# Attention, routed experts and a rational feed-forward layer on one core: gates, weight loads and a pipeline's lag moved

## The chip, the cores and the metric

The kernel runs on one core of a Trainium2 chip. The metric is the device time of one execution in microseconds (us); lower is better. A time is the median of several executions, and one more execution is taken by the hardware profiler.

## The reference

Three layers follow each other on 3072 tokens of 512 numbers, all in fp32.

```python
# 1 attention: chunks of 32 queries see 16 keys to the left, 8 to the right and 8 memory slots
a = softmax(scale * q_c @ k_full.T);  out = a @ v_full
# 2 experts: 8 of them, one per token
logits = x @ w_gate + modality_bias[modality_id]
e_idx = argmax(logits);  gate_w = softmax(logits)[e_idx]
h = maximum(x[mask] @ w1[e], 0);  out[mask] = gate_w[mask, None] * (h @ w2[e])
# 3 feed-forward with a rational function
h = x @ w_in                                   # 512 -> 2048
g = (a0 + a1*h + a2*h*h + a3*h**3) / (1 + |b0|*|h| + |b1|*h*h + 1e-6)
out = g @ w_out                                # 2048 -> 512
```

`w_in` and `w_out` come as float64 and are narrowed on the chip.

## The kernel before, in words

Attention and the router fill the first 150 us. They sort the tokens by expert into slots of 128.

**Experts.** `moe` handles 20 slots as five quads of four slots (512 tokens); I call them the first to the fifth quad (`q` 0 to 4). A quad runs eight steps, `n` 0 to 7, one for each 128 hidden units. In a step TensorE (PE) does 12 products of the first layer (`mm1_quad`, lines 1018 to 1020), ScalarE (ACT) takes the ReLU (`hh`, line 1025) and VectorE (DVE) the low half (`hl`, line 1026); PE then does the 12 products of the second layer of the step before (`mm2_quad`, lines 1035 to 1037). Every fp32 operand is split in a high and a low part, so each product is three matmuls.

While a quad runs, the next one is prepared. POOL gathers its four slots of x (`gather`, line 807) into the buffers `xy`. ACT scales each by the token's gate (`gate_x`, line 907). At `n` = 7 PE transposes the first two of them (`prep_x`, line 1081) ahead of `mm2_quad(6)`, and the other two behind it; ACT and DVE write the result into `xq` (lines 1083 and 1085), which the next quad's first product reads. SP loads the next expert's weights, if the expert changes, in four pairs of 512 KB, one pair in each of four steps (`load_w`, line 820); ACT and DVE split them (`split_w`, lines 917 and 920).

The first and the fourth quad also carry a small extra slot of 32 rows (`k` is not `None`) with an expert of its own: its weights are loaded raw in the steps 0 to 3, two pieces of `w1r` or `w2r` a step, its first layer runs at `n` = 3 (`mm1_small`, line 856) and its second at `n` = 4 (`mm2_small`, line 872).

Beside all this runs the **converter**, which narrows `w_in` and `w_out`, one piece of 128 x 512 at each call of `filler()`. One call issues the end of the last piece (a cast on ACT, line 1326, a subtraction on DVE, line 1327, and for `w_out` two stores from POOL, lines 1329 and 1330), the load of the next piece on SP (line 1313, 512 KB into `wr`, two buffers) and the bits of this piece (line 1259 on ACT and four operations on DVE, lines 1260 to 1263).

The order of all instructions is that of the program text: `manual_schedule` keeps it, and each engine takes its own in that order. Inside a step the text has first `mm1_quad` and the ReLU, then at `n` = 7 the first transposes, then `mm2_quad`, then `at(n)`:

```python
        def at(n):
            if n in FILLERS[q]:
                filler()
            ...                                       # the small slot's loads, load_w
            if n >= NC8 - 2 and len(nxt) > 1:         # NC8 is 8
                for c in nxt[0:2] if n == NC8 - 2 else nxt[2:4]:
                    ex.gate_x(c)
```

**Feed-forward.** `moe2` runs 96 steps, six blocks of 512 tokens by 16 pieces of 128 hidden units. Step `i` has 12 matmuls of the first layer on PE (`mm1`, lines 1402 to 1404), the rational function on ACT and DVE, whose results are `gh` (ACT, line 1438) and `gl` (DVE, line 1444), and the second layer (`mm2`, lines 1459 to 1461), which does nothing for an even piece and 24 matmuls for two pieces after an odd one. `mm2` of step `i - LAG` stands behind `mm1` of step `i`, and `LAG` is 3. A block's sums lie in four PSUM banks and are copied out by `evac` (lines 1467 to 1472) and stored by POOL (line 1474).

Of the kernel before, what the change touches and what calls it, by code (L numbers as in the profile page):

```python
# [13 lines left out]
F32R = mybir.dt.float32r  # L14
# [8 lines left out]
P = 128  # L23
# [322 lines left out]
NC8 = 1024 // P  # L346
# [3 lines left out]
class Router:  # L350
# [137 lines left out]
    def gates(self, lo, hi):  # L488

        V = self.nc.vector  # L490
        a = slice(lo, hi)
        L, g = self.L[:, a], self.v[:, 4, a]
        return [
            lambda: V.reduce_sum(g, L, axis=AX.X),
            lambda: V.tensor_scalar_add(g, g, 1e-9),
            lambda: V.reciprocal(g, g),
        ]
# [605 lines left out]
FILLERS = (range(8), range(6), range(6), (0, 4, 5, 6, 7), range(8))  # L1103


def moe(nc, tc, ex, filler, rows, gp):
    ET = mybir.EngineType
    flags, w1r = ex.flags, ex.w1r
    gate0 = gp.tile([P, QUAD * P], F32, name="gate0")
    small = gp.tile([P, 4, SM], F32, name="small_y")  # L1110

    def quad(q):
        c0 = Q_FIRST + QUAD * q
        nxt = range(c0 + QUAD, c0 + 2 * QUAD) if q + 1 < QUADS else range(S_LAST, S_LAST + 1)
        k = QUAD_SMALL.get(q)
        pieces = {0: (1, 0), 1: (1, 2), 2: (2, 0), 3: (2, 2)}
        loads = {n if k is None else n + 4: x for n, x in pieces.items()}
        part1, part2 = (5, 6) if k is None else (6, 7)
        sx, (sh, sT) = ex.xy[3], [x[:, 0:256] for x in ex.xg[0:2]]
        sT = sT[:, 0:P].rearrange("p (k n) -> p k n", k=4)  # L1120
        hT = ex.xg[0][:, 256:512].rearrange("p (i n) -> p i n", i=2)
        if k is not None:
            e = ex.expert(NS - 1 - k)

        def at(n):

            if n in FILLERS[q]:
                filler()
            if k is not None and n in pieces:
                layer, i = pieces[n]  # L1130
                ex.load(e, layer, range(i, i + 2))
            if n in loads:
                layer, i = loads[n]
                ex.load_w(nxt[0], layer, range(i, i + 2))
            if n == part1:
                ex.split_w(nxt[0], 1, range(2))
            if n == part2:
                ex.split_w(nxt[0], 2, range(2))
            if n == (2 if k is None else 5):
                for c in nxt:  # L1140
                    ex.gather(c)
            if n >= NC8 - 2 and len(nxt) > 1:
                for c in nxt[0:2] if n == NC8 - 2 else nxt[2:4]:
                    ex.gate_x(c)

        for n in range(NC8):
            ps = ex.mm1_quad(n)
            if n == 0 and q == 0:
                ex.mm2(EARLY, 0)
                ex.put(1, ex.turn(1))  # L1150
                ex.mm2(EARLY, 1)
                ex.out(EARLY)
            if n == 1 and q == 0:
                ex.put(EARLY, ex.turn(EARLY))
                ex.gate_row(Q_FIRST, gate0)
            ex.relu_quad(n, ps)
            if n == 0 and q == 0:
                ex.load_w(Q_FIRST, 2)
                ex.split_w(Q_FIRST, 2)
            if k is not None and n == 0:  # L1160
                ex.gather_small(k, sx[:, 0:D_M])
            if k is not None and n == 3:
                ex.prep_x_small(sx, sT)
            if k is not None and n == 4:
                ex.prep_h_small(sh, hT)
            if k is not None and n == 5:
                ex.put_small(k, sx[:, 0:D_M], small)
            if n == NC8 - 1:
                xs = [(c, ex.prep_x(c, c - nxt[0] if len(nxt) > 1 else None)) for c in nxt[0:2]]
                for c, low in xs:  # L1170
                    low()
            if n > 0:
                ex.mm2_quad(n - 1)
            if k is not None and n == 3:
                ex.mm1_small(sT, sh)
            if k is not None and n == 4:
                ex.out_small(k, ex.mm2_small(hT), sx)
            at(n)
        for c in nxt[2:]:
            ex.prep_x(c, c - nxt[0])()  # L1180
        ex.split_w(nxt[0], 1, range(2, 4))
        if q + 1 == QUADS:
            while filler():
                pass
            rows.open()
            for t in range(4):
                rows.load(0, t, w1r[:, t, 0:TB])
            for part in range(3):
                ex.mm1(S_LAST, part)
            ex.hs = ex.w2r[:, 0].rearrange("p (i j n) -> p i j n", i=2, j=4)  # L1190
            ex.relu(S_LAST)
            ex.mm2_quad(NC8 - 1, range(2))
            ex.prep_h(S_LAST, 0)
        ex.mm2_quad(NC8 - 1, range(2, 4) if q + 1 == QUADS else range(QUAD))
        ex.put_quad(c0, gate0 if q == 0 else None)
        ex.split_w(nxt[0], 2, range(2, 4))

    def first_y(t):
        rows.prep(t, w1r[:, t, 0:TB], rows.h, rows.l)

    filler()
    ex.split_w(EARLY, 2)
    for q in range(QUADS):
        quad(q)
    ex.prep_h(S_LAST, 1)
    for t in range(4):
        first_y(t)
    for k in range(SMALL - 1, -1, -1):
        ex.copy_small(k)
    ALL = (ET.PE, ET.Activation, ET.DVE, ET.Pool, ET.SP)  # L1210
    more = nc.values_load(flags[0:1, 2, 0:1], engines=ALL, min_val=0, max_val=1)
    tc.mark_branch_hint_location("more", "LikelyTaken", engines=(ET.PE, ET.Activation))
    for g in range(2):
        ex.mm2(S_LAST, g)
    with tc.If(more == 1, label="more"):
        ex.clear_columns(w1r[:, 0])
        for i in range(Q_FIRST, NN):
            if i == S_LAST or i < S_LAST and (i - Q_FIRST) % QUAD == 0:
                continue
            todo = nc.values_load(flags[0:1, 2, i:i + 1], engines=ALL, min_val=0, max_val=1)  # L1220
            with tc.If(todo == 1):
                e = ex.expert(i)
                for layer in (1, 2):
                    ex.load(e, layer)
                    ex.split_w(i, layer, always=True)
                nc.gpsimd.memset(ex.xg[i % QUAD], 0.0)
                ex.gather(i)
                ex.prep_x(i)()
                for part in range(3):
                    ex.mm1(i, part)  # L1230
                ex.relu(i)
                ex.prep_h(i, 0)
                ex.prep_h(i, 1)
                for part in range(2):
                    ex.mm2(i, part)
                ex.out(i)
                ex.merge(i)
        for t in range(4):
            rows.load(0, t, w1r[:, t, 0:TB])
        for t in range(4):  # L1240
            first_y(t)
    ex.out(S_LAST, y=rows.spare, ps=ex.pb[1])
# [2 lines left out]
DM, DF = 512, 2048  # L1245
NB = 6
TB = 512
LAG = 3
NF = DF // P
NK = DM // P  # L1250
F_MIN = float(np.array(0x38000000, np.uint32).view(np.float32))
# [116 lines left out]
def moe2(nc, tc, rows, wih, wil, wod, consts, out):  # L1368
    with ExitStack() as ctx:
        cp = ctx.enter_context(tc.tile_pool(name="c_c", reuse_waits="tile", bufs=1))  # L1370
        rp = ctx.enter_context(tc.tile_pool(name="c_r", reuse_waits="tile", bufs=2))
        wk = ctx.enter_context(tc.tile_pool(name="c_w", reuse_waits="tile", bufs=2))
# [19 lines left out]
        def prep_y(blk, k):  # L1392
            rows.prep(k, yr.pop((blk, k)), *yT[blk % 2])
# [40 lines left out]
            V.scalar_tensor_tensor(out=u, in0=u, scalar=a0, in1=q, op0=ALU.add, op1=ALU.mult)  # L1434

        def ew_hi(i):
            gh = wk.tile([P, TB], F32R, tag="gh", name="gh", bufs=4)
            A.copy(gh, u_t[i])  # L1438
            g_t[i] = gh

        def ew_lo(i):
            gl = wk.tile([P, TB], F32R, tag="gl", name="gl", bufs=4)
            gh = g_t[i]
            V.tensor_tensor(out=gl, in0=u_t.pop(i), in1=gh.bitcast(F32), op=ALU.subtract)  # L1444
            g_t[i] = (gh, gl)
# [38 lines left out]
        n = len(steps)  # L1484
        for i in range(n + LAG):
            if i < n:
# [8 lines left out]
            if 2 <= i <= n + 1:  # L1495
                ew_lo(steps[i - 2])
            if i >= LAG:
                mm2(*steps[i - LAG])
            if i < n:
                ew_act1(steps[i])  # L1500
            if 1 <= i <= n:
                ew_dve2(steps[i - 1])
                ew_hi(steps[i - 1])
            if i < n:
# [4 lines left out]
                if blk + 1 < NB:  # L1509
                    if f in (4, 6, 9, 11):  # L1510
                        load_y(blk + 1, (f - 3) // 2 - f // 9)
                    if f in (8, 10, 12, 14):
                        prep_y(blk + 1, (f - 8) // 2)
            if i >= LAG and steps[i - LAG][1] == NF - 1:
                evac(steps[i - LAG][0])

# [99 lines left out]
```

## Time and profile before

| | |
|---|---|
| median of 3 runs | 949.23 us (948.18 to 950.88) |
| the profiled execution | 950.31 us |
| its span, first to last instruction | 948.6 us |
| mean granted TensorE clock | 0.996 of full |
| PE busy | 916.0 us, 97% |
| DVE busy | 743.3 us, 78% |
| ACT busy | 546.4 us, 58% |
| POOL busy | 150.9 us, 16% |

Times in rows count from the span's start. A group of instructions with a number in brackets behind it has that much idle time of its engine ahead of it, and the arrow names what ended the idle time. A matmul's end is modelled and its duration overlaps the next one's, so lengths on PE are taken from start to start.

### The profile page before, as it was taken

What the parts mean: (1) busy time and instruction counts of PE and PEld (TensorE: products, weight loads), DVE (VectorE), ACT (ScalarE), POOL (GpSimd) and SP (SyncE); (2) the same over time, 40 slices, a digit from 0 to 9 for tenths busy, and PEclk for the clock granted to TensorE, in tenths of its full rate; (3) what the DMA queues carried; (4) which work ended last, traced back from release to release, by engine and by line L of the source; (5) the groups of instructions that cost most, each with busy time, mean ns of one, the idle gap of its engine ahead of it and who ended that gap; (6) DMA issues with size and microseconds to landing.
All of it is one profiled execution on the core that took longest, in us unless ns stands there. A gap on an engine that the chain in (4) does not pass through costs nothing.

```text
span 948.6 us, 15349 instructions
## 1 busy us (share of the span) xinstructions
PE 916.0 (97%) x5684; PEld 744.7 (79%) x5684; DVE 743.3 (78%) x1244; ACT 546.4 (58%) x913; POOL 150.9 (16%) x198
## 2 busy tenths in 40 slices
PE   6999899999999999999999999999999999999997
PEld 5786578688887778877888888888888888888885
DVE  6777693377767266549999899899999998998884
ACT  3554433243737153257777676777766776767663
POOL 5111221031121043114631000100010010001001
PEclk9999999999999999999999999999999999999999
DMA  8999633459293676556851000100010010001001
GB/s 320 360 386 354 216 101 121 157 167 324 83 339 121 236 225 206 204 189 95 124 65 62 1 23 22 45 12 23 12 45 23 23 45 1 23 1 45 1 1 44
DMA packets 37814, 114.90 MB, mean 121 GB/s; under 512 B 8987, under 2 KB 9119, under 8 KB 34912
## 3 DMA queue, kind: packets, MB, share of 16 engines
q1 hardware_dynamic: 25920, 79.06, 27.1%
q0 software_dynamic: 11488, 33.85, 9.9%
q8 instruction: 46, 0.75, 0.3%
q10 hardware_dynamic: 320, 0.91, 0.3%
q14 instruction: 40, 0.33, 0.1%
HBM read 86.51 MB, written 27.54 MB: 120 GB/s over the span
## 4 chain that ended last, share of the span: by engine, by line
issue 55%; PE 26%; POOL 7%; DMA 6%; DVE 4%; ACT 1%; POOLq 1%; ACTq 0%; DVEq 0%; SPq 0%
POOL od L897 3%; DMA yd<-xy 2%; PE pv L210 2%; PE pa L154 2%; PE hq L1018 2%; POOL out L1474 2%; PE hq L1019 2%; PE hq L1020 2%; DMA wr<-in_moe_w_out 2%; PE pps L188 1%; PE pb L1096 1%; PE pa L949 1%; PE xps L234 1%; PE pb L1035 1%; PE pb L1037 1%
## 5 line engine op out<-in xcount | busy, mean ns | idle before, releaser
L1459 PE MATMUL a<-wo,gh 128*128 128x512 f32 x384 | 149.6, 390 | 1.6 <-ACT gh L1438 1.6
L1461 PE MATMUL a<-wo,gl 128*128 128x512 f32 x384 | 149.6, 390 | 1.3 <-DVE gl L1444 1.3
L1402 PE MATMUL h<-yh,wih 128*128 128x512 f32 x384 | 149.6, 389 | 0.8 <-ACT wf L956 0.8
L1404 PE MATMUL h<-yh,wil 128*128 128x512 f32 x384 | 149.4, 389 | 0.0
L1403 PE MATMUL h<-yl,wih 128*128 128x512 f32 x384 | 149.4, 389 | 0.0
L1460 PE MATMUL a<-wo,gh 128*128 128x512 f32 x384 | 149.4, 389 | 0.0
L1414 ACT ACTIVATE s<-h 128x512 f32<-128x512 f32 x96 | 56.6, 590 | 105.4 <-PE h L1404 105.4
L1421 DVE SCALAR_TENSOR_TENSOR q<-s,ab,q 128x512 f32<-128x512 f32 x96 | 71.8, 748 | 38.0 <-ACT q L1415 38.0
L1474 POOL DMA_INDIRECT out<-o,out_rows x24 | 25.4, 1060 | 426.4 <-ACT o L1470 419.7
L1438 ACT CAST gh<-u 128x512 fp32r<-128x512 f32 x96 | 59.9, 624 | 45.3 <-DVE u L1434 41.4
L1459 PEld LDWEIGHTS a<-wo,gh 128*128 128x128 f32 x384 | 72.1, 188 | 17.3 <-ACT gh L1438 2.5
L1461 PEld LDWEIGHTS a<-wo,gl 128*128 128x128 f32 x384 | 72.0, 187 | 17.0 <-DVE gl L1444 2.1
L1402 PEld LDWEIGHTS h<-yh,wih 128*128 128x128 f32 x384 | 72.0, 188 | 16.0 <-ACT wf L956 1.2
L1404 PEld LDWEIGHTS h<-yh,wil 128*128 128x128 f32 x384 | 72.2, 188 | 15.1
L1460 PEld LDWEIGHTS a<-wo,gh 128*128 128x128 f32 x384 | 72.2, 188 | 14.8
L1403 PEld LDWEIGHTS h<-yl,wih 128*128 128x128 f32 x384 | 72.0, 188 | 14.9
L1416 ACT ACTIVATE u<-h,ab 128x512 f32<-128x512 f32 x96 | 74.9, 780 | 0.0
L1434 DVE SCALAR_TENSOR_TENSOR u<-u,ab,q 128x512 f32<-128x512 f32 x96 | 72.2, 752 | 3.4
L1423 DVE SCALAR_TENSOR_TENSOR u<-u,ab,h 128x512 f32<-128x512 f32 x96 | 71.8, 748 | 3.4
L1432 DVE SCALAR_TENSOR_TENSOR q<-q,ab,s 128x512 f32<-128x512 f32 x96 | 71.6, 745 | 1.7 <-ACT s L1428 1.7
L1427 ACT ACTIVATE s<-q,ab 128x512 f32<-128x512 f32 x96 | 70.1, 730 | 1.1
L1433 DVE SCALAR_TENSOR_TENSOR q<-q,s 128x512 f32<-128x512 f32 x96 | 66.4, 692 | 3.3
(308 smaller groups left out, 1785.9 us busy)
## 6 DMA issues: line engine op xcount, KB each, us to landing
in<-in_qkv SPq DMA_DIRECT2D x22, 560.0 KB
in<-in_qkv SPq DMA_DIRECT2D x22, 556.0 KB
w1r<-in_moe_w SPq DMA_DIRECT2D x20, 512.0 KB
w2r<-in_moe_w SPq DMA_DIRECT2D x20, 512.0 KB
wr<-in_moe_w_in SPq DMA_DIRECT2D x16, 512.0 KB
wr<-in_moe_w_out SPq DMA_DIRECT2D x16, 512.0 KB
wod<-wo POOLq DMA_DIRECT2D x32, 256.0 KB
wo<-wod SPq DMA_DIRECT2D x16, 512.0 KB
```

The lines of the kernel that those rows point to most:

```text
L1402: nc.tensor.matmul(ps, lhsT=wih[k][:, sl], rhs=h[:, k], start=(k == 0), stop=False)
L1403: nc.tensor.matmul(ps, lhsT=wih[k][:, sl], rhs=l[:, k], start=False, stop=False)
L1404: nc.tensor.matmul(ps, lhsT=wil[k][:, sl], rhs=h[:, k], start=False, stop=(k == NK - 1))
L1416: A.activation(u, ps, func=AF.Identity, scale=a3, bias=a2)
L1421: V.scalar_tensor_tensor(out=q, in0=s, scalar=absb1, in1=q, op0=ALU.mult, op1=ALU.add)
L1423: V.scalar_tensor_tensor(out=u, in0=u, scalar=a1, in1=ps, op0=ALU.add, op1=ALU.mult)
L1427: A.activation(s, q, func=AF.Ln, bias=cb)
L1432: V.scalar_tensor_tensor(out=q, in0=q, scalar=cb, in1=s, op0=ALU.add, op1=ALU.mult)
L1434: V.scalar_tensor_tensor(out=u, in0=u, scalar=a0, in1=q, op0=ALU.add, op1=ALU.mult)
L1459: nc.tensor.matmul(ps, lhsT=gh[:, sl], rhs=wo[x][:, 0].bitcast(F32R), start=(x == 0), stop=False)
L1460: nc.tensor.matmul(ps, lhsT=gh[:, sl], rhs=wo[x][:, 1].bitcast(F32R), start=False, stop=False)
L1461: nc.tensor.matmul(ps, lhsT=gl[:, sl], rhs=wo[x][:, 0].bitcast(F32R), start=False, stop=(x == NF - 1))
```

## The change

Four things move. The gates are issued directly behind a ReLU and the next products, no longer at the end of `at(n)`: for quads with a small slot at `n` = 6 (two slots) and, behind the first transposes of `n` = 7, the other two; for quads without one at `n` = 5 and `n` = 6. In `at(n)` the loads of experts' weights come ahead of the converter's call. `LAG` goes from 3 to 4. `gh` and `gl` get six buffers each.

```diff
@@ quad @@
+        gate1 = 5 if k is None else 6
+
+        def gates(cs):
+            for c in cs:
+                ex.gate_x(c)
+
@@ at(n) @@
-            if n in FILLERS[q]:
-                filler()
             if k is not None and n in pieces:
                 layer, i = pieces[n]
                 ex.load(e, layer, range(i, i + 2))
             if n in loads:
                 layer, i = loads[n]
                 ex.load_w(nxt[0], layer, range(i, i + 2))
+            if n in FILLERS[q]:
+                filler()
@@
-            if n >= NC8 - 2 and len(nxt) > 1:
-                for c in nxt[0:2] if n == NC8 - 2 else nxt[2:4]:
-                    ex.gate_x(c)
@@ the loop over n @@
             ex.relu_quad(n, ps)
+            if len(nxt) > 1 and n == gate1:
+                gates(nxt[0:2])
+            if len(nxt) > 1 and n == gate1 + 1 and k is None:
+                gates(nxt[2:4])
@@
                 for c, low in xs:
                     low()
+                if k is not None:
+                    gates(nxt[2:4])
@@ moe2 @@
-LAG = 3
+LAG = 4
-            gh = wk.tile([P, TB], F32R, tag="gh", name="gh", bufs=4)
+            gh = wk.tile([P, TB], F32R, tag="gh", name="gh", bufs=6)
-            gl = wk.tile([P, TB], F32R, tag="gl", name="gl", bufs=4)
+            gl = wk.tile([P, TB], F32R, tag="gl", name="gl", bufs=6)
```

The changed kernel's lines from 1119 on have numbers up to 9 higher. In the rows below `wr` is the converter's raw buffer.

On SP, in the first quad, before, the steps `n` = 2 and `n` = 3:

```order
L1313 DMA wr_2322<-in_moe2_w_in 128x1024
L820 ISA
L820 DMA w2r_93<-in_moe_w2 128x2x512
L820 ISA
L820 DMA w2r_93<-in_moe_w2 128x2x512
L1313 DMA wr_2322<-in_moe2_w_in 128x1024
L820 ISA
L820 DMA w2r_93<-in_moe_w2 128x2x512
L820 ISA
L820 DMA w2r_93<-in_moe_w2 128x2x512
```

Now, from the converter's load of `n` = 1 to that of `n` = 3:

```order
L1322 DMA wr_2322<-in_moe2_w_in 128x1024
L820 ISA
L820 DMA w2r_93<-in_moe_w2 128x2x512
L820 ISA
L820 DMA w2r_93<-in_moe_w2 128x2x512
L1322 DMA wr_2322<-in_moe2_w_in 128x1024
L820 ISA
L820 DMA w2r_93<-in_moe_w2 128x2x512
L820 ISA
L820 DMA w2r_93<-in_moe_w2 128x2x512
L1322 DMA wr_2322<-in_moe2_w_in 128x1024
```

Each pair of the small slot's pieces stands one converter load earlier in SP's queue.

On ACT, in the fourth quad, before, from the ReLU of `n` = 6 (`hh`) to the gates of the next quad's first two slots (`xy_89`, `xy_86`); the rows from 924 to 930 are a branch over a split that is not taken there:

```order
L1025 ACTIVATE hh_1762<-hq 128x512
L1326 CAST wo<-wr 128x512
L1259 ACTIVATE wf<-wr 128x512
L924 TENSOR_LOAD flags
L924 ISA x2
L930 COMPARE_AND_BRANCH
L917 CAST w1h<-w1r 128x4x256 x2
L930 UNCONDITIONAL_BRANCH x2
L907 ACTIVATE xy_89<-xy_89,gate_s 128x512
L834 UNCONDITIONAL_BRANCH
L907 ACTIVATE xy_86<-xy_86,gate_s 128x512
```

Now:

```order
L1025 ACTIVATE hh_1762<-hq 128x512
L907 ACTIVATE xy_89<-xy_89,gate_s 128x512
L907 ACTIVATE xy_86<-xy_86,gate_s 128x512
L1335 CAST wo<-wr 128x512
L1268 ACTIVATE wf<-wr 128x512
```

The gates have passed the converter's two instructions, and a wait for the gathered rows now stands ahead of those.

On PE, at the start of the feed-forward stage, before, the end of the fifth `mm1` (`h_8703`) and the start of the first `mm2` (`a0_8684`):

```order
L1404 MATMUL h_8703<-yh0_4965,wil2_2316 128x512
L1402 MATMUL h_8703<-yh0_4965,wih3_2313 128x512
L1403 MATMUL h_8703<-yl0_4966,wih3_2313 128x512
L1404 MATMUL h_8703<-yh0_4965,wil3_2317 128x512
L1459 MATMUL a0_8684<-wo0_8450,gh_8629 128x512
L1460 MATMUL a0_8684<-wo0_8450,gh_8629 128x512
```

Now, the end of the fifth `mm1` (`h_8699`) and the start of the sixth (`h_8737`):

```order
L1413 MATMUL h_8699<-yh0_4965,wil2_2316 128x512
L1411 MATMUL h_8699<-yh0_4965,wih3_2313 128x512
L1412 MATMUL h_8699<-yl0_4966,wih3_2313 128x512
L1413 MATMUL h_8699<-yh0_4965,wil3_2317 128x512
L1411 MATMUL h_8737<-yh0_4965,wih0_2310 128x512
L1412 MATMUL h_8737<-yl0_4966,wih0_2310 128x512
```

A sixth `mm1` of 12 matmuls stands ahead of the first `mm2`; at the end of the stage, accordingly, three `mm2` follow each other with no `mm1` between them, where two did.

## Rows read from the trace of the kernel before

**Rows 1.** The page, busy time, share and instructions of each engine.
```profile
PE 916.0 (97%) x5684; PEld 744.7 (79%) x5684; DVE 743.3 (78%) x1244; ACT 546.4 (58%) x913; POOL 150.9 (16%) x198
```

**Rows 2.** Waits of PE: line, releaser, us in total, times, longest; feed-forward's second layer.
```profile
PE a L1459 <- ACT gh L1438: 1.6, 2, 0.9
PE a L1461 <- DVE gl L1444: 1.3, 1, 1.3
```

**Rows 3.** PE's timeline and windows, small slots, `n` = 4; columns: busy of engines, PEclk, DMA.
```profile
181.54 1.08 PE L872 MATMUL syp<-w2r,xy 128*32 128x128 f32 x32
184.12 0.65 PE L872 MATMUL syp<-w2r,xy 128*32 128x128 f32 x16 [1.50 <-DMA w2r<-in_moe_w]
...
330.63 1.95 PE L872 MATMUL syp<-w2r,xy 128*32 128x128 f32 x64
...
181.54:190.54 9.00, 6.82 (x77) 4.92 (x76) 2.18 (x5) 2.58 (x6) 0.00 (x0) 0.81 0.25 80
330.63:335.46 4.83, 4.83 (x78) 3.86 (x77) 0.71 (x2) 2.56 (x6) 0.45 (x1) 1.00 0.01 3
```

**Rows 4.** Timeline of SP, first quad, n = 2 and n = 3.
```profile
167.43 0.97 SPq L820 DMA_DIRECT2D w2r<-in_moe_w  x2
...
178.04 0.95 SPq L820 DMA_DIRECT2D w2r<-in_moe_w  x2
```

**Rows 5.** Timeline of PE, ACT and SP, end of the third quad.
```profile
295.23 1.36 PE L1081 MATMUL xps<-ident,xy 128*128 128x128 f32 x8 [1.76 <-ACT xy L907]
...
288.97 0.67 ACT L1259 ACTIVATE wf<-wr 128x512 f32<-128x512 f32 x1 [3.01 <-DMA wr<-in_moe_w_out]
...
280.71 0.35 SPq L1313 DMA_DIRECT2D wr<-in_moe_w_out  x1
```

**Rows 6.** Timelines and a window, end of the fourth quad; the last two rows end the second.
```profile
340.25 1.07 POOL L807 DMA_INDIRECT xy<-xd,src_u  x1 [0.30 <-issue]
...
343.08 0.66 ACT L1326 CAST wo<-wr 128x512 fp32r<-128x512 f32 x1 [0.83 <-DVE wr L1263]
...
344.49 0.34 SPq L1313 DMA_DIRECT2D wr<-in_moe_w_out  x1
...
345.74 1.36 ACT L907 ACTIVATE xy<-xy,gate_s 128x512 f32<-128x512 f32 x2 [0.60 <-DMA xy<-xd,src_u]
...
350.43 0.66 ACT L1259 ACTIVATE wf<-wr 128x512 f32<-128x512 f32 x1 [1.21 <-DMA wr<-in_moe_w_out]
...
352.36 1.64 PE L1081 MATMUL xps<-ident,xy 128*128 128x128 f32 x8 [1.66 <-ACT xy L907]
...
354.66 0.69 DVE L1085 TENSOR_TENSOR xq<-xps,xq 128x512 fp32r<-128x512 f32 x1 [0.20 <-ACT xq L1083]
...
357.90 0.40 PE L1018 MATMUL hq<-xq,w1h 128*128 128x512 f32 x1
...
350.00:375.00 25.00, 23.34 (x100) 19.02 (x99) 15.72 (x27) 10.42 (x18) 7.50 (x13) 0.93 0.63 205
...
251.52 1.12 PE L1081 MATMUL xps<-ident,xy 128*128 128x128 f32 x8
...
255.23 0.39 PE L1018 MATMUL hq<-xq,w1h 128*128 128x512 f32 x1
```

**Rows 7.** Timeline of PE and DVE, start of the feed-forward stage.
```profile
429.49 0.39 PE L1459 MATMUL a<-wo,gh 128*128 128x512 f32 x1
...
437.64 0.39 PE L1402 MATMUL h<-yh,wih 128*128 128x512 f32 x1
...
443.08 0.39 PE L1459 MATMUL a<-wo,gh 128*128 128x512 f32 x1
...
427.66 0.68 DVE L1444 TENSOR_TENSOR gl<-u,gh 128x512 fp32r<-128x512 f32 x1
...
432.48 0.68 DVE L1444 TENSOR_TENSOR gl<-u,gh 128x512 fp32r<-128x512 f32 x1
```

**Rows 8.** Timeline of PE and DVE, end of the feed-forward stage.
```profile
935.40 0.39 PE L1459 MATMUL a<-wo,gh 128*128 128x512 f32 x1
...
941.92 0.39 PE L1461 MATMUL a<-wo,gl 128*128 128x512 f32 x1
```

## The prediction

> **What bounds the kernel now.** I read the page's engine list first. PE is busy 97% of the span and DVE 78% [rows 1], so PE sets the end and only what shortens, lengthens or idles PE counts. So next I read PE's idle groups and, around each, the timelines of PE and of the engine that ended the wait. Behind the router stage three places lose time that an edit of this change touches: the small slot's second layer in the first quad waits for its weights [rows 3, 4]; the transposes at the end of the third and of the fourth quad wait for ACT's gates [rows 5, 6]; the feed-forward stage waits for `gh` and `gl` three times, 2.9 us in all, and never again in its 96 steps [rows 2]. In [rows 7, 8] the reader sees where those three are. The clock is the last thing to see: around the fourth quad's end the granted clock is 0.93 over 25 us [rows 6], so the wait there cost more than its own length.
>
> **Loads ahead of the converter.** The small slot's second layer is 64 matmuls, and from their start to the next transposes PE takes 9.00 us in the first quad and 4.83 in the fourth [rows 3]. The same work, so 4.17 us are lost in the first. The row names 1.50 of them as a wait for `w2r`; the granted clock of that stretch is 0.81 against 1.00, so PE also ran part of it at its lower level, 1.2 GHz, behind the stall [rows 3]. What it waits for is the pair issued at 178.04; the pair before was issued at 167.43 [rows 4]. SP was held between them by the converter's load, which needs a free `wr`. In the order of the change that load stands behind the pair, so the last pair goes out where the one before it did, some 10.6 us earlier; even at the 8.26 us that the longest load of my rows took (280.71 to 288.97) [rows 5] it has landed by 176, ahead of 181.54. **-4.17**, nothing if the pair cannot go earlier. The converter's load comes two issues (1 us) later; it has a step to land, see the slower rival. In the other quads PE waited for no pair: 0.
>
> **Gates, third quad.** PE stood 1.76 us at 295.23 for the gates on ACT, while ACT had idled 3.01 us ahead of 288.97, waiting for a load [rows 5]. The first two gates (1.36 us for two [rows 6]) now go into `n` = 5, where their rows have long landed, and fit into that idle time. **-1.76.** The second quad's boundary took 3.71 us from transpose to first product without a wait (251.52 to 255.23) [rows 6]: 0 there.
>
> **Gates, fourth quad.** The boundary ran from 350.70 (352.36 less 1.66 of wait) to 357.90, 7.20 us against 3.71 undisturbed [rows 6]: 3.49 to win, half of it the wait, half the lower clock behind it. But the gates now stand ahead of the converter's cast on ACT and wait for the gather. The gather was issued at 340.25 and ACT could start at 345.74, until 347.10; the cast had run at 343.08 [rows 6]. So it goes 4.0 later, and with it SP's load, from 344.49 to 348.5. The load took 5.94 to its use at 350.43 [rows 6]; behind that use stand DVE's bits and then the last low half of `xq`, which ended at 355.35, 4.92 behind. If the whole delay is passed on, the use is at 354.4 and the quad starts at 359.3, 1.4 later than before; with the wait comes the lower clock, another 1.8 (3.49 less 1.66): **+3.0** at worst, rounded. If the load is quicker by what a quiet queue may give (use at 351.7, hardly more than 3 us behind its issue), the low half ends at 356.6, and PE starts 1.3 to 1.5 earlier: **-1.5** at best. I take **0**, the middle, as ACT's wait goes and DVE's comes.
>
> The gather of 128 rows took 5.49 us from issue to use (340.25 to 345.74) [rows 6]. The Trainium skill, "DMA: Bandwidth & Descriptors", section "Anatomy of one DMA — SWDGE (gpsimd) path", fits about 2.0 us plus bytes over 436 GB/s per transfer issued from POOL; that makes an estimate of 2.6 us for 256 KB, half of the row. By that rule the gates would be through about when the cast began, the converter would be some 1 us late, and this term -1.5 and the time 938.0. The row decides: 5.49.
>
> **Gates, first quad.** The same reorder, on a boundary that did not wait for gates. Its rows can land late too; if not, the gates' own 1.36 us [rows 6] come ahead of the cast. From 0 to +1.4; I take **+0.2**, since ACT is busy 58% of the span [rows 1] and mostly has the room.
>
> **LAG, start.** From the first `mm2` at 429.49 to the next `mm1` at 437.64 are 8.15 us, and the same 24 matmuls in the next step take 5.44 (437.64 to 443.08) [rows 7]. The 2.71 between are waits for `gh` and `gl` and what follows them. With the sixth `mm1` ahead, 12 matmuls or 2.72 us of the same work are put in front. The first `gl` was there at 432.48 + 0.68 = 433.16 [rows 7]; its first reader is then at 429.49 + 2.72 + 5 x 0.227 = 433.34. A slack of 0.17 only, but it grows: DVE gives one `gl` every 4.82 us (427.66 to 432.48) [rows 7] and PE takes 5.44. **-2.71**; 0.5 less if `gl` is that much late. Each `gh` and `gl` lives a step longer, and six buffers instead of four give that room and one more, so nothing waits for a free one: 0.
>
> **LAG, end.** The last `mm2` from 935.40 to 941.92 took 6.52 us for 23 starts, at 0.2267 each 5.21 [rows 8]: the last results were late. Now another `mm2` stands before it and hides that: **-1.31**. What follows, the copies out and the stores, keeps its length: 0. `evac` comes a step later, on banks that the next block needs a step later too: 0.
>
> **Sum.** -4.17 - 1.76 + 0 + 0.2 - 2.71 - 1.31 = -9.75. The profiled execution took 950.31, so 940.6; it lies 1.08 above the median of 949.23, so **939.5** against the median.
>
> **Rivals.** *Late boundaries.* The fourth quad loses 3.0 and the first 1.4 in place of 0 and 0.2: 943.7. For: ACT's new wait stands ahead of the cast. Against: the load may land sooner. 0.16.
>
> *Early gathers.* The gates' rows lie there when ACT comes, by 343.1, and the converter's load lands in 5 us; then the fourth boundary is undisturbed and gains up to its 3.49: 936.0 to 938.0. Against: the 5.49 us of [rows 6]. 0.09.
>
> *The pair does not move.* If the raw buffer of the last pair is still read when SP comes to it, the 4.17 stay: 943.7. Against: the fourth quad runs the same two layers out of the same buffers without a wait [rows 3]. 0.05. *Two at once*, this and the late boundaries: 947.9, no change that can be told. 0.06.
>
> *Slower: the converter starves.* Its load now stands directly behind a pair of 1 MB. A load had 8.26 us issue to use (280.71 to 288.97), shortly behind pairs, and 5.94 (344.49 to 350.43) with none near [rows 5, 6], 2.32 more. It has a step, 5.44 us [rows 7], and ACT's next ReLU stands behind it; PE needs that only 12 matmuls (2.72) later. So from 8.16 us per load, step after step, PE stops. Over the 13 steps with both, half of 2.32 reaching PE gives 15 us: 954.5. For: one row is already above 8.16. Against: the pairs were ahead of that load before as well, and PE did not stop for it; they come in 13 steps, never together. 0.06.
>
> **How the numbers follow.** Forecast 0.58, its own range 938 to 941.5 (fourth quad -1.5 to +1.5, `gl` 0.5). A measurement can tell about 0.3%, 2.8 us. Faster by more: forecast, late boundaries, early gathers, unmoved pair, 0.88; within it: two at once, 0.06; slower: 0.06. Range 935.8 to 943.8: it takes in all but the last two and the edges.
>
> **What would show it.** Right: in the first quad `syp` runs without a wait for `w2r`, some 4.8 us to the next group; no wait for `xy` at the third quad's transposes; at the fourth's end the gates run at about 345.7 with the cast behind them, and PE waits for `xq`, not for ACT's gates; the start of feed-forward has no wait for `gh` or `gl`, and its last `mm2` takes 5.2. Wrong: a wait of PE for `hh` or for the converter's `wf` in many steps (starving), a wait for `w2r` as before, or `mm2` waiting for `gl` in mid-stage.

## The result: 1.0% faster, 0.9899 of the time before

The changed kernel takes 940.75 us (median of 6 runs, 939.40 to 942.37) against 951.15 of the kernel before in the same comparison; the ratio is 0.9899 (0.9882 to 0.9916), which on the median of 949.23 is 939.6. The profiled execution took 939.40 with a span of 937.8, 10.8 less than before. The page of the kernel after, busy time of each engine:

```profile
PE 911.8 (97%) x5684; PEld 742.7 (79%) x5684; DVE 742.8 (79%) x1244; ACT 547.2 (58%) x913; POOL 149.8 (16%) x198
```

The work is the same as in [rows 1]; PE is busy 4.2 us less, which fits its granted clock (0.999 on average, 0.996 before), and idle 6.6 us less. The waits of PE in what this change touches, kernel after (line, releaser, us, times, longest):

```profile
PE hq L1019 <- DVEq L930: 2.7, 2, 2.3
```

The two groups of [rows 2] are gone, and so are the waits for `w2r` and for ACT's `xy` of [rows 3, 5, 6]; one new group is there: the second matmul of a quad waits for DVE.

**The small slot.** Timeline and window of PE, kernel after, first quad, `n` = 4 (window: length, busy time of PE, PEld, DVE, ACT, POOL, granted clock, DMA share, GB/s):

```profile
181.07 1.95 PE L872 MATMUL syp<-w2r,xy 128*32 128x128 f32 x64
185.90 0.43 PE L964 MATMUL yps<-ident,xy 32*128 32x32 f32 x4
...
181.07:185.90 4.83, 4.83 (x77) 3.86 (x77) 0.71 (x2) 2.56 (x6) 0.00 (x0) 1.00 0.00 1
```

The 64 matmuls run in one piece at full clock, 4.83 us to the next group as in the fourth quad of [rows 3]. SP, kernel after: the last pair of `w2r` is issued at 167.04, where before it was 178.04 [rows 4].

```profile
161.96 0.98 SPq L820 DMA_DIRECT2D w2r<-in_moe_w  x2
166.43 0.35 SPq L1322 DMA_DIRECT2D wr<-in_moe_w_in  x1
167.04 0.95 SPq L820 DMA_DIRECT2D w2r<-in_moe_w  x2
```

**The fourth boundary.** Timelines of POOL, ACT, DVE and PE, kernel after:

```profile
334.11 1.06 POOL L807 DMA_INDIRECT xy<-xd,src_u  x1 [0.30 <-issue]
...
339.15 1.46 ACT L907 ACTIVATE xy<-xy,gate_s 128x512 f32<-128x512 f32 x2 [3.04 <-DMA xy<-xd,src_u]
340.52 0.65 ACT L1335 CAST wo<-wr 128x512 fp32r<-128x512 f32 x1
...
346.19 0.69 ACT L1268 ACTIVATE wf<-wr 128x512 f32<-128x512 f32 x1 [0.91 <-DMA wr<-in_moe_w_out]
...
349.83 1.29 DVE L1085 TENSOR_TENSOR xq<-xps,xq 128x512 fp32r<-128x512 f32 x2 [0.49 <-DVEq L930]
...
348.49 0.39 PE L1018 MATMUL hq<-xq,w1h 128*128 128x512 f32 x1
351.18 0.50 PE L1019 MATMUL hq<-xq,w1h 128*128 128x512 f32 x1 [2.30 <-DVEq L930]
```

The gates wait 3.04 us for the gather on ACT, the cast stands behind them, and the chain of [rows 6] runs later: load, `wf` at 346.19, DVE's bits, the last low halves until 351.12. PE has its transposes and starts the quad at 348.49, but its second matmul reads the low half and waits 2.30. The profile names a branch of DVE (`DVEq L930`) as the releaser; the last low half ended at 351.12, 0.06 ahead of PE's start, and the run filler_behind below shows that it is this that PE waits for.

**The third boundary.** Timelines of SP, ACT and PE, kernel after:

```profile
277.80 0.35 SPq L1322 DMA_DIRECT2D wr<-in_moe_w_out  x1
...
279.73 1.33 ACT L907 ACTIVATE xy<-xy,gate_s 128x512 f32<-128x512 f32 x2
...
282.91 0.66 ACT L1268 ACTIVATE wf<-wr 128x512 f32<-128x512 f32 x1 [0.45 <-DMA wr<-in_moe_w_out]
...
289.29 1.11 PE L1081 MATMUL xps<-ident,xy 128*128 128x128 f32 x8
```

PE's transposes have no wait ahead of them. ACT's gates ran early, but the converter's load also came sooner: ACT waits 0.45 us for it where it waited 3.01 [rows 5]. Which of the two ended PE's wait the experiments must tell.

**Feed-forward.** Timeline of PE, kernel after, its first `mm2`, the `mm1` behind it, and the last `mm2`:

```profile
425.31 0.39 PE L1468 MATMUL a<-wo,gh 128*128 128x512 f32 x1
...
430.80 0.39 PE L1411 MATMUL h<-yh,wih 128*128 128x512 f32 x1
...
925.84 0.39 PE L1468 MATMUL a<-wo,gh 128*128 128x512 f32 x1
...
931.05 0.39 PE L1470 MATMUL a<-wo,gl 128*128 128x512 f32 x1
```

5.49 us in place of 8.15 [rows 7], and 5.21 for the last in place of 6.52 [rows 8].

**Lengths by stage.** PE runs 5684 matmuls in every kernel here, up to feed-forward the same ones in the same order, so I cut all traces at the same matmuls, from start to start: the small slot from the 2251st to the 2321st, the first boundary 2361st to 2441st, the start of the second quad to the 2561st, the third boundary 2741st to 2831st, the fourth 3081st to 3161st, feed-forward's first 96 matmuls (from the 3377th), and its tail from the 5661st to the end of the span. The table has the profiled execution of every run, in us:

| kernel | small slot | 1st boundary | 2nd quad's start | 3rd boundary | 4th boundary | ff start | tail |
|---|---|---|---|---|---|---|---|
| before | 11.99 | 17.52 | 27.20 | 20.93 | 20.15 | 24.18 | 13.25 |
| after | 7.82 | 17.80 | 27.20 | 18.77 | 19.47 | 21.50 | 11.93 |
| lag_alone | 12.02 | 17.52 | 27.20 | 20.26 | 20.64 | 21.49 | 11.93 |
| loads_alone | 7.82 | 17.51 | 27.20 | 18.77 | 20.53 | 24.20 | 13.25 |
| gates_alone | 12.07 | 17.69 | 27.20 | 19.76 | 21.29 | 24.18 | 13.25 |
| four_buffers | 7.82 | 17.73 | 27.20 | 18.77 | 19.28 | 21.49 | 11.93 |
| loads_and_lag | 7.82 | 17.50 | 27.20 | 18.77 | 20.73 | 21.49 | 11.93 |
| filler_behind | 7.81 | 17.14 | 27.67 | 18.77 | 16.82 | 21.52 | 11.92 |
| filler_behind_again | 7.82 | 17.14 | 27.59 | 18.77 | 16.93 | 21.49 | 11.93 |
| filler_behind_late_gates | 7.82 | 17.14 | 27.56 | 18.77 | 17.41 | 21.48 | 11.93 |
| small_loads_alone_ahead | 7.82 | 17.73 | 27.20 | 19.32 | 21.15 | 21.49 | 11.93 |
| changed_again | 7.82 | 17.69 | 27.20 | 18.77 | 19.47 | 21.51 | 11.93 |
| lag_five | 7.82 | 17.68 | 27.20 | 18.77 | 19.61 | 22.02 | 11.93 |

The other cuts from the 1901st matmul on agree within 0.1 us in all kernels, but for 0.28 in one stretch of the third quad of the changed kernel and 5.18 in lag_five's feed-forward. The way to the 1901st matmul, attention and router, takes 120.3 to 128.5 us with no relation to the edits; it is why ratios scatter by some 0.3%, and why I read stages. Most stages repeat to a tenth of a microsecond. Boundaries with a long wait do not: `before` and `lag_alone` run the same program up to feed-forward and differ by 0.67 at the third boundary and 0.49 at the fourth, and the kernels that are alike at the fourth (`after`, `changed_again`, `four_buffers`, `lag_five`) lie between 19.28 and 19.61. One execution of each kernel stands in the table, so smaller differences there tell nothing.

### The profile page after: what moved, and what is told of

The parts are those of the page before. It is cut to its first block, busy times and chain, and to the rows that moved or that the text cites. A ratio compares the mean times of both kernels' runs of the same rounds, so it can differ in the third digit from the quotient of the medians.

```text
span 937.8 us, 15345 instructions
## 1 busy us (share of the span) xinstructions
PE 911.8 (97%) x5684; PEld 742.7 (79%) x5684; DVE 742.8 (79%) x1244; ACT 547.2 (58%) x913; POOL 149.8 (16%) x198
## 4 chain that ended last, share of the span: by engine, by line
issue 44%; DVE 9%; PE 6%; POOL 2%; ACT 1%; POOLq 0%; DVEq 0%; ACTq 0%
POOL out L1483 2%; DVE u L1443 2%; DVE q L1442 1%; DVE q L1441 1%; DVE q L1430 1%; DVE gl L1453 1%; DVE u L1431 1%; PE hq L1019 1%; PE hq L1020 1%; PE hq L1018 1%; PE pb L949 1%; PE hps L1096 1%; PE pb L1037 0%; PE pb L1036 0%; PE pb L1035 0%
```

## The experiments

My theory after the result: each part acts at its own place and the parts add up. The first rivals put a gain down to another part than the one that was named for it.

**lag_alone**

```diff
-LAG = 3
+LAG = 4
```

with six buffers of `gh` and `gl`.

> The kernel before with LAG 4 and six buffers of gh and gl, nothing else. Theory (each part acts at its own place and the parts add up): the three waits for gh and gl go, the feed-forward stage is 4.0 us shorter, ratio to before 0.9958 (0.3 to 0.5% less); the waits at 184, 295 and 352 us stay as they were. Rival (the feed-forward stage gains only because the experts' stage hands over differently): under 1 us, ratio 0.999 or more.

Ratio 0.9955 (0.9935 to 0.9975); the start of feed-forward is 2.69 shorter, the tail 1.32. The theory holds for feed-forward and the rival falls. The waits at the two boundaries stay, but not at their lengths of 1.76 and 1.66 us. PE, LAG alone, third and fourth boundary:

```profile
299.14 1.36 PE L1081 MATMUL xps<-ident,xy 128*128 128x128 f32 x8 [1.09 <-ACT xy L907]
...
356.96 1.77 PE L1081 MATMUL xps<-ident,xy 128*128 128x128 f32 x8 [2.31 <-ACT xy L907]
```

Nothing ahead of feed-forward was changed in this run, so that much is scatter.

**loads_alone**

```diff
-            if n in FILLERS[q]:
-                filler()
...
                 ex.load_w(nxt[0], layer, range(i, i + 2))
+            if n in FILLERS[q]:
+                filler()
```

> The kernel before with the experts' loads ahead of the converter's call, nothing else. Theory: the wait for w2r in the first quad goes with the lower clock behind it, 4.1 us, ratio 0.9957; the boundaries of the third and the fourth quad keep their 1.8 and 1.7 us of wait for the gates. Rival (the converter's loads, now behind the pairs, land later and eat part of it in the second and third quad): 2 us or less, ratio 0.998 or more, with waits of PE that were not there before.

Ratio 0.9929 (0.9905 to 0.9953), more than either expected. The small slot is 4.17 shorter. But the third boundary is 2.16 shorter too, as short as in the changed kernel, with the gates where they were. In [rows 5] the converter's load of 280.71 stood directly behind a pair of the next expert's weights. SP, before:

```profile
279.03 1.00 SPq L820 DMA_DIRECT2D w2r<-in_moe_w  x2
```

SP and ACT, loads alone, the same load and the step that uses it:

```profile
273.50 1.00 SPq L820 DMA_DIRECT2D w2r<-in_moe_w  x2
277.61 0.35 SPq L1313 DMA_DIRECT2D wr<-in_moe_w_out  x1
...
281.65 0.35 SPq L1313 DMA_DIRECT2D wr<-in_moe_w_out  x1
...
285.60 0.66 ACT L1326 CAST wo<-wr 128x512 fp32r<-128x512 f32 x1 [1.97 <-issue]
286.38 0.69 ACT L1259 ACTIVATE wf<-wr 128x512 f32<-128x512 f32 x1
...
291.34 1.34 ACT L907 ACTIVATE xy<-xy,gate_s 128x512 f32<-128x512 f32 x2
```

The load of 281.65 has another converter load between itself and the last pair, and its use, `wf` at 286.38, follows the cast without the 3.01 us of wait. ACT is no longer late, and the gates are through in time. So my theory falls in one point: the parts do not add up at the third boundary.

**gates_alone.** The kernel before with the gates at their new places; the edit is the gates' part of the change.

> The kernel before with the gates directly behind the ReLU, nothing else. Theory: the third quad's boundary gains 1.8 us and the fourth's about 1.0, the first's stays, so 2.8 us, ratio 0.9970; the 1.5 us wait for w2r in the first quad stays. Rival (the fourth quad's gain comes from the loads' new place): 1.8 us or less, ratio 0.998 or more, and the fourth boundary as long as before, 7.2 us or more.

Ratio 0.9998 (0.9980 to 1.0017): nothing. The rival's number is nearer: against `before`, 1.17 won at the third boundary, 1.14 lost at the fourth, 0.17 at the first; against `lag_alone`, 0.50 won and 0.65 lost at the same two. SP and ACT, gates alone, third quad:

```profile
284.61 1.00 SPq L820 DMA_DIRECT2D w2r<-in_moe_w  x2
286.15 5.78 SPq L1322 DMA_DIRECT2D wr<-in_moe_w_out  x2
...
295.31 0.67 ACT L1268 ACTIVATE wf<-wr 128x512 f32<-128x512 f32 x1 [4.48 <-DMA wr<-in_moe_w_out]
```

The converter's load, issued right behind the pair, took 9.16 us to its use, as the one of [rows 5] took 8.26. ACT is late whether the gates stand ahead of it or not; now the low half of the hidden values is late, and the third boundary keeps 0.60 of wait for it. At the fourth, PE, gates alone:

```profile
356.15 0.72 PE L1081 MATMUL xps<-ident,xy 128*128 128x128 f32 x4 [0.28 <-DVE hl L1026]
...
362.15 0.73 PE L1019 MATMUL hq<-xq,w1h 128*128 128x512 f32 x1 [2.28 <-DVEq L930]
362.68 0.63 PE L1020 MATMUL hq<-xq,w1l 128*128 128x512 f32 x1
```

The same wait of 2.3 as in the changed kernel, and behind it matmuls of 0.63 instead of 0.39: PE's lower level, 1.2 GHz. Windows around the wait, gates alone, then the kernel after:

```profile
350.00:375.00 25.00, 22.45 (x99) 18.05 (x98) 16.30 (x28) 12.51 (x22) 7.19 (x13) 0.93 0.71 210
```

```profile
340.00:365.00 25.00, 22.55 (x106) 18.54 (x105) 18.80 (x32) 13.50 (x23) 7.31 (x13) 1.00 0.70 223
```

Granted clock 0.93 against 1.00. That is most of the difference between 21.29 and 19.47: one wait, with and without the clock's fall; the wait of 0.28 for the hidden values is the rest.

**four_buffers**

```diff
-            gh = wk.tile([P, TB], F32R, tag="gh", name="gh", bufs=6)
+            gh = wk.tile([P, TB], F32R, tag="gh", name="gh", bufs=4)
```

and the same for `gl`, in the changed kernel.

> The changed kernel with four buffers of gh and gl instead of six. Theory (the buffers are room that nothing needs for the time: ACT and DVE only run less far ahead): as the changed kernel, ratio to before 0.990, no wait of PE for gh or gl. Rival (four buffers tie ACT to the second layer two steps later, the slack at the start does not grow and PE waits again): 2 us or more back, ratio 0.992 or more, with waits for gh or gl in the stage.

Ratio 0.9898 (0.9871 to 0.9925), both feed-forward cuts as with six. The buffers are not needed.

**loads_and_lag.** The changed kernel without the gates' part. The theory was mended by then: the loads end the third quad's wait.

> The changed kernel with the gates where they were before: loads ahead of the converter and LAG 4 with six buffers. Theory now (the loads alone end the third quad's wait, and the early gates are worth only what they win at the fourth boundary, about 1 us): first quad's small slot 7.82 us, third boundary as in the changed kernel, fourth boundary with a wait for the gates of 1.7 to 2.3 us and 1.0 us longer than in the changed kernel; 0.7 to 1.0 us above the changed kernel, ratio to before 0.990 to 0.991. Rival (the prediction's own split: the gates are what ends the third quad's wait): 1.8 us of wait at the third boundary, 2.5 us or more above the changed kernel, ratio 0.9925.

Ratio 0.9886 (0.9856 to 0.9917), below what both expected, but its interval does not tell it from the changed kernel. The stages decide: third boundary 18.77, no wait there; fourth 20.73. PE, fourth boundary, loads and LAG:

```profile
351.27 0.97 PE L1081 MATMUL xps<-ident,xy 128*128 128x128 f32 x4 [2.41 <-ACT xy L907]
```

The mended theory holds. By these stages the early gates are worth 1.26 at the fourth boundary (0.9 to 1.45 with the scatter there) and cost 0.30 at the first; the whole times are too close to show it.

**filler_behind.** In the first and the fourth quad the converter's last call moves behind the last transposes:

```diff
-            if n in FILLERS[q]:
+            if n in FILLERS[q] and not (k is not None and n == NC8 - 1):
                 filler()
...
             ex.prep_x(c, c - nxt[0])()
+        if k is not None:
+            filler()
```

> The changed kernel, in which the converter's call of the last step of the first and the fourth quad stands behind the last transposes and their low halves instead of ahead of them. Theory (what PE waits for there, 2.30 and 0.35 us, is DVE with the converter's bits ahead of the low half of xq): both waits go, 2.5 us less than the changed kernel, ratio to before 0.987. Rival (the next quad's first converter step is late instead, or the store of its results is): under 1 us, ratio 0.989 or more, with a wait at the fifth quad's first steps.

Ratio 0.9876 (0.9836 to 0.9917), an interval that holds both; the stages don't: 2.65 less at the fourth boundary, 0.66 less at the first, 0.47 more at the start of the second quad, where a little comes back. No wait at the fifth quad's first steps. PE's wait was for the low halves behind the converter's bits. DVE and PE, filler behind, fourth boundary:

```profile
352.66 2.71 DVE L1085 TENSOR_TENSOR xq<-xps,xq 128x512 fp32r<-128x512 f32 x4
...
356.20 0.39 PE L1018 MATMUL hq<-xq,w1h 128*128 128x512 f32 x1
356.43 0.39 PE L1019 MATMUL hq<-xq,w1h 128*128 128x512 f32 x1
```

The four low halves follow each other and are done at 355.37, ahead of the quad's first product, and its second has no wait.

**filler_behind_late_gates.** The same with the gates where they were.

> As the run with the filler behind the transposes, but with the gates where they were before. Theory (the late gates at the fourth boundary wait for the converter's load of the last step, so moving that call behind also frees them; the early gates are then worth nothing): the same time as with early gates within 0.5 us, ratio 0.987, no wait for gates of over 0.5 us. Rival (they wait for the gather and for the step before): a wait of PE for the gates at the fourth boundary remains, 1 us or more above.

Ratio 0.9878 (0.9848 to 0.9908). Between the two: 0.59 longer at the fourth boundary than with early gates, with 0.67 of wait for ACT's gates. So even there the converter's call was most of what the gates had waited for, and the gather the rest.

**small_loads_alone_ahead**

```diff
-            if n in FILLERS[q]:
-                filler()
...
             if k is not None and n in pieces:
                 layer, i = pieces[n]
                 ex.load(e, layer, range(i, i + 2))
+            if n in FILLERS[q]:
+                filler()
             if n in loads:
```

> The changed kernel, but only the small slot's loads stand ahead of the converter's call; the next expert's loads stand behind it as before. Theory (a converter load that is issued directly behind the pair of the step ahead of it is the one that makes ACT late at the third boundary): the first quad's small slot still takes 7.82 us, the third boundary is longer than in the changed kernel by about 1 us and the converter's last load there takes over 8 us from issue to use again, ratio 0.991. Rival (only the small slot's loads matter): as the changed kernel in every stage, ratio 0.990.

Ratio 0.9914 (0.9881 to 0.9948). The small slot keeps its 7.82. The third boundary is 0.55 longer than in the changed kernel. SP and ACT there:

```profile
279.06 1.00 SPq L820 DMA_DIRECT2D w2r<-in_moe_w  x2
280.58 5.90 SPq L1322 DMA_DIRECT2D wr<-in_moe_w_out  x2
...
288.99 0.67 ACT L1268 ACTIVATE wf<-wr 128x512 f32<-128x512 f32 x1 [3.62 <-DMA wr<-in_moe_w_out]
```

8.41 us from issue to use again, with 3.62 of wait. The place of the next expert's pairs is what makes this load late; with early gates it costs half of the microsecond that I expected. The fourth boundary, 21.15, has the lower clock again behind 2.12 of wait.

**changed_again and filler_behind_again**

> The changed kernel once more, beside the next two on the same chip: ratio to before 0.990, as on record, and by stage the same lengths within 0.3 us but for the attention ahead of the experts, which differs by some us from one execution to the next.

> The run with the filler behind the transposes once more, to compare it directly with the changed kernel. Theory: 2.8 us less by stages (2.65 at the fourth boundary, 0.2 around the first), ratio to before about 0.003 lower than the changed kernel's. Rival: what is won at the boundaries comes back in the stages behind them, no difference.

0.9902 (0.9871 to 0.9933) and 0.9855 (0.9824 to 0.9886); 941.84 and 938.19 in the median. By stages the second is 2.70 less (2.54 at the fourth boundary, 0.55 at the first, less 0.39 behind it). The intervals of the ratios still touch; all five of its runs (937.54 to 938.79) lie below all six of the changed kernel (940.37 to 945.29). It is the fastest kernel of this study.

**lag_five**

```diff
-LAG = 4
+LAG = 5
-            gh = wk.tile([P, TB], F32R, tag="gh", name="gh", bufs=6)
+            gh = wk.tile([P, TB], F32R, tag="gh", name="gh", bufs=7)
```

> The changed kernel with LAG 5 and a seventh buffer of gh. Theory (LAG 4 has ended every wait for gh and gl, with 0.18 us left at the first reader): nothing more to win, the same time within 0.5 us, the 24 matmuls of a step 5.44 us long at the start and at the end. Rival (a wait is left that the trace puts on no releaser, or the longer tail costs something): 1 us or more either way.

Ratio 0.9944 (0.9921 to 0.9967), 4 us worse than LAG 4. The rival's number, but neither theory's mechanism. PE, then ACT, at the change from the first block of tokens to the second:

```profile
484.65 0.49 PE L1411 MATMUL h<-yh,wih 128*128 128x512 f32 x1 [2.02 <-ACT yh L1299]
486.12 0.50 PE L1412 MATMUL h<-yl,wih 128*128 128x512 f32 x1 [0.98 <-DVE yl L1300]
486.46 0.42 PE L1413 MATMUL h<-yh,wil 128*128 128x512 f32 x1
486.70 0.61 PE L1468 MATMUL a<-wo,gh 128*128 128x512 f32 x1
```

```profile
483.46 0.62 ACT L1447 CAST gh<-u 128x512 fp32r<-128x512 f32 x1 [1.03 <-DVE u L1443]
483.98 0.61 ACT L1299 CAST yh<-yr 128x512 fp32r<-128x512 f32 x1
```

The second block's first layer now stands one second layer earlier on PE than with LAG 4. ACT casts its inputs between two steps of the rational function, at 483.98. PE waits 3.0 us and falls to the lower clock (matmuls of 0.61); with that the stage is 5.18 longer. It happens there alone: the four later changes of block have no such wait.

## Why the prediction was right, and where only its sum was

The time (939.5 forecast, 939.6 by the ratio) and the sum (-9.75, against -10.4 from the 1901st matmul on in the two profiles) were right. By its steps:

- *Loads ahead*, -4.17: the small slot is 4.17 shorter, in every run that has the edit and in none that lacks it.
- *Gates, third quad*, -1.76: **this step failed as a cause.** The boundary did lose 2.16, but the loads alone win all of it, and the gates alone 0.50 to 1.17. The prediction took the gates' place on ACT for what made them late. It had the better reading in the same rows: the 3.01 us of wait ahead of 288.97, for a load of 8.26 us issued just behind a pair [rows 5]. That row went into the slower rival as a danger of the new order; it was the fault of the old one. The prediction added a gain to the wrong part, and its number came out right by luck, as both parts are in the change.
- "In the other quads PE waited for no pair: 0", in the step on the loads: true of the waits' names and false of the effect. A pair made the converter late, the converter ACT, and ACT the gates.
- *Gates, fourth quad*, 0 (-1.5 to +3.0): -0.68. The mechanism is as described: the gates wait until 339.15, 5.04 us behind the gather's issue, the cast goes later, and the last low half ends 4.93 behind `wf`, where 4.92 was used. The converter's load took 4.27 us from issue to use (341.92 to 346.19), between the prediction's two bounds, 5.94 and some 3; no row shows the 3. The prediction's worst case adds 1.4 and 1.8, which is 3.2 and not 3.0. The estimate of 2.6 us for the gather, from the Trainium skill's fit for a transfer issued from POOL ("DMA: Bandwidth & Descriptors", "Anatomy of one DMA — SWDGE (gpsimd) path"), is not borne out by this case's traces: they have 5.04 and, before, 5.49. So the measurement was the one to use. What was not in the middle value is the clock: with the same wait of 2.3 the boundary took 19.28 to 19.61 where the clock stayed and 21.15 to 21.29 where it fell.
- *Gates, first quad*, +0.2: +0.17 to +0.28, with 0.25 to 0.35 of wait for the low half.
- *LAG, start*, -2.71: -2.68. The slack at the first reader of `gl`, 0.17 forecast, was 0.18: `gl` ended at 426.27 and its reader began at 426.45.
- *LAG, end*, -1.31: -1.32.
- *Six buffers*, "give that room and one more, so nothing waits for a free one: 0": nothing waits, and with four nothing that reaches PE either. They were no condition.
- *The slower rival* did not come. In the steps with pairs a converter load still took up to 8.8 us (issued at 260.81, landed at 269.57 in the changed kernel), as it said, and PE did not wait for it; the load of the third quad that counted came sooner: 5.11 us from issue to use (277.80 to 282.91) in place of 8.26.

Of the sum, what the parts alone give by stages is -4.0 (LAG, feed-forward only), -6.0 (loads) and +0.1 (gates), the last two with the scatter of the old boundaries in them. The gates are worth a microsecond only together with the loads, and that by stages alone.

## What to carry to other kernels

A wait's name is its last link: before an edit is credited with ending it, follow the releaser one engine further back, and ask whether another edit of the same change ends the same chain. On an in-order queue, what must wait for a buffer (here a load for `wr`) should stand behind what need not, and an engine's optional work behind what the next stage reads. A pipeline's lag moves every due time with it: one step more ended PE's waits for `gh` and `gl`, and two steps made the inputs of the next block the late ones.

## What the runs showed that I had not expected

- The same wait of PE, 2.1 to 2.3 us at the same instruction, was followed by PE's lower level (1.2 GHz) in some kernels and not in others: of those with early gates and the converter's call ahead, the changed kernel (twice), four_buffers and lag_five kept the clock, gates_alone and small_loads_alone_ahead lost it, at a cost of 1.5 to 2.0 us. A short wait for the low half of the hidden values comes 6 us earlier in both that lost it, but in lag_five as well. What does divide them is the loads' place: the kernels that kept the clock have the next expert's pairs ahead of the converter's call, and the two that lost it have them behind. So the rival of gates_alone may be right in this, that the loads' new place is a condition of the fourth boundary's gain; with one or two executions of each kernel and no mechanism seen, what decides it stays open.
- The converter's load of 512 KB whose use is late in [rows 5] took 8.1 to 9.2 us from issue to use where it stood directly behind a pair of 1 MB on the same queue (before, lag_alone, gates_alone, small_loads_alone_ahead), and 4.4 to 5.5 in the nine other executions, which have a converter load between them.
- The attention ahead of the experts varied by 8 us between profiled executions, more than any part of the change moves.
